# Attention and two expert layers on one core: the first layer's first expert chosen after four tiles, and zeros stored later

## The chip, the core and the metric

The kernel runs on one NeuronCore of a Trainium2 chip. Its engines are TensorE (PE, with its weight loads shown as PEld), VectorE (DVE), ScalarE (ACT), GpSimd (POOL) and SyncE (SP); each works off its own queue in program order, and they wait for each other by semaphores. Sixteen transfer (DMA) engines move data between HBM and the on-chip memory. The metric is the device time of one launch in microseconds.

## What is computed

A linear attention with decay over two sequences of 768 tokens and 8 heads, and two mixture-of-experts layers over the 1536 rows that it gives, with 8 experts of 512 x 1024 x 512 and one expert per row.

```python
state = gamma[None, :, None, None] * state + np.einsum('bhd,bhe->bhde', k[:, :, t], v[:, :, t])
y[:, :, t] = scale * np.einsum('bhd,bhde->bhe', q[:, :, t], state)
...
logits = x @ w_gate
expert_idx = np.argmax(logits, axis=1)
...
h = np.maximum(xe @ w1[e], 0.0)
ye = h @ w2[e]
out[mask] = gate_w[mask, None] * ye
```

The second layer does the same with weights of its own, and keeps at most `capacity` = 384 rows per expert.

## The kernel before

**Attention** goes over twelve tiles of 128 tokens (`n` from 0 to 11, alternating between the two sequences): scores, the state's update, the output `xt` from past and present, and `combine`, which transposes a tile's output back to rows and makes the gate's logits. ScalarE's queue stores each tile's rows and logits into the HBM tensor `x1d` (`a_store`).

**Routing** finds for every row its expert and its rank among that expert's rows. The first eight tiles do this in batches (`BATCHES`: five tiles and three), whose steps `pick`, `count`, `rank`, `slots` and `place` are set by hand between the tiles' steps; the last four tiles go one by one (`route_tile`). `run` keeps running counts. After eight tiles `early` gathers the first 128 rows of one expert, the "first" one, so that products with it can start before attention has ended. Before, layer 1's first expert is expert 0 by decree; layer 2's is the one with most rows by then (`choose`, which leaves a mask `one`, a bonus `first` and a floor `floor`, and the number in `chosen`; `of_first` picks that expert's column with the mask).

**An expert layer** is eight slots, each an expert with a fixed number of columns (`CAPS`), wide slots first: `finish_route` sorts the experts by their counts, with the first expert pinned to slot 0 by its bonus. If an expert has more rows than its slot, a conditional block at the end of the program does the rest. Slot 0 makes its hidden products with undivided weights (`whole`, line L429), 128 columns ahead of the others: the first batch from the rows of `early`, the second (`second`, from line L370's transposes on) when the remaining rows have been gathered with the index list `ig`. All else uses weights split in a high part `whi` (ScalarE, L163) and a rest `wlo` (VectorE or GpSimd, L174): 32 pairs of products per slot for the hidden side (L788 and L789) and 32 for the output side (L814 and L815).

**Weights** are loaded on SP's queue in pieces of 512 KB (`refill` into four buffers `st`, `load_whole`); a piece can be loaded when its buffer's last piece has been split. `know` gives the list of pieces an expert's number, fixed or read into a register of SP. The loads of slot 1 wait until the second gather of slot 0 has landed (`held`).

**`x2d`**, the rows of layer 2, has to be zero where layer 1 gives nothing. SP stores twelve tiles of zeros into it behind the last weight load of attention, and layer 1's scatters wait for them. `between(j, i)` is what stands beside part `i` (0 to 7) of slot `j`.

## Time and profile before

| | |
|---|---|
| median of 3 runs | 442.85 us (441.76 to 446.3) |
| profiled execution | 443.88 us; span 442.1 us, 1.8 us around it |
| PE | 411.3 us busy, 93% of the span |
| VectorE, ScalarE, GpSimd | 74%, 54%, 29% of the span |
| transfers | 100.50 MB, 227 GB/s in the mean |
| attention, with first products | to 71.7 us |
| slot 0 of layer 1 | from 77.5 to 98.9 us |
| layer 2 | from some 265 us on |

All times are from the start of the span. A row of the timeline gives start, length, engine, line, operation, output from inputs, and in brackets how long the engine stood idle before and what it waited for. The granted clock is the share of TensorE's full clock, 2.4 GHz, that was passed in a stretch; 0.50 is 1.2 GHz.

### The profile page before, as it was taken

The page shows a single profiled execution, that of the slowest core. Times are in us where ns is not written, and L with a number is a line of the kernel's source. Part 1 is how long each engine was busy: PE and PEld are TensorE (multiplying, and loading weights), DVE is VectorE, ACT ScalarE, POOL GpSimd, SP SyncE. Part 2 cuts the span into 40 slices and gives each one's busy share as a digit, 9 for nine tenths or more (in the row PEclk, how much of TensorE's full clock was granted, in tenths as well). Part 3 has the DMA queues.
Part 4 walks back from the last instruction along what each step waited for, and adds up shares of the span by engine and source line. Part 5 has one row for each costly group of instructions (what it writes and reads, how often), then busy time and mean ns, then how long its engine had stood idle before and what let it go on. Part 6 is the DMA issues. An engine that isn't in the chain of part 4 may idle for free.

```text
span 442.1 us, 9412 instructions
## 1 busy us (share of the span) xinstructions
PE 411.3 (93%) x3373; PEld 384.4 (87%) x3373; DVE 325.3 (74%) x858; ACT 239.2 (54%) x493; POOL 127.0 (29%) x102
## 2 busy tenths in 40 slices
PE   8999884998999999999999999998999999999980
PEld 7887674998899999999989898997888999999970
DVE  3658896177989898989899877187586877887830
ACT  2111240266757666667666651366676777878730
POOL 2443113033353535344442204003202303201020
PEclk9999999799999999999999999999999999999996
DMA  8998994628575766666665733559758677777510
GB/s 317 391 310 300 380 387 148 215 97 264 189 257 169 240 212 241 215 234 220 231 218 191 266 128 89 231 191 313 271 184 269 221 261 249 256 245 247 188 43 14
DMA packets 32854, 100.50 MB, mean 227 GB/s; under 512 B 5008, under 2 KB 5520, under 8 KB 32800
## 3 DMA queue, kind: packets, MB, share of 16 engines
q1 hardware_dynamic: 25488, 82.75, 54.1%
q0 software_dynamic: 5008, 13.06, 8.8%
q10 hardware_dynamic: 2304, 4.02, 2.4%
q8 instruction: 28, 0.46, 0.4%
q14 instruction: 26, 0.21, 0.2%
HBM read 87.08 MB, written 13.05 MB: 226 GB/s over the span
## 4 chain that ended last, share of the span: by engine, by line
PE 59%; DVE 16%; DMA 10%; issue 9%; ACT 2%; POOL 1%; POOLq 0%; SPq 0%; ACTq 0%; DVEq 0%
PE y L814 14%; PE h L788 13%; PE y L815 6%; PE h L789 6%; DVE wlo L174 5%; PE h L429 4%; PE cb L1277 4%; DMA vk<-vkr 2%; DMA whole<-w 2%; DVE hs L774 2%; PE tp L359 2%; DVE h L800 2%; DMA rows<-x1d,eig 2%; DVE rkey L209 2%; PE o L829 1%
## 5 line engine op out<-in xcount | busy, mean ns | idle before, releaser
L174 DVE TENSOR_TENSOR wlo<-st,whi 128x1024 fp32r<-128x1024 f32 x107 | 141.2, 1328 | 0.9 <-ACT whi L163 0.9
L163 ACT CAST whi<-st 128x1024 fp32r<-128x1024 f32 x120 | 124.8, 1045 | 25.4 <-DMA st<-w 24.5
L788 PE MATMUL h<-x,whi 128*128 128x416 f32 (+10 forms) x416 | 123.5, 364 | 0.0
L814 PE MATMUL y<-h,whi 128*128 128x416 f32 (+8 forms) x384 | 117.6, 370 | 0.0
L789 PE MATMUL h<-x,wlo 128*128 128x208 f32 (+10 forms) x416 | 104.5, 251 | 0.0
L815 PE MATMUL y<-h,wlo 128*128 128x208 f32 (+8 forms) x384 | 97.3, 253 | 0.0
L788 PEld LDWEIGHTS h<-x,whi 128*128 128x128 f32 x416 | 78.1, 188 | 2.5 <-issue 0.4
L789 PEld LDWEIGHTS h<-x,wlo 128*128 128x128 f32 x416 | 79.5, 191 | 0.1
L814 PEld LDWEIGHTS y<-h,whi 128*128 128x128 f32 x384 | 72.1, 188 | 2.4 <-issue 0.2
L815 PEld LDWEIGHTS y<-h,wlo 128*128 128x128 f32 x384 | 73.4, 191 | 0.0
L174 POOL TENSOR_TENSOR wlo<-st,whi 128x1024 fp32r<-128x1024 f32 x13 | 34.9, 2684 | 57.7 <-ACT whi L163 51.3
L318 POOL DMA_INDIRECT out<-ob,is x14 | 13.9, 995 | 114.8 <-ACT ob L835 111.1
L800 DVE SCALAR_TENSOR_TENSOR h<-hs,h 128x416 fp32r<-128x416 f32 (+10 forms) x52 | 29.0, 558 | 20.7 <-ACT h L799 17.9
L799 ACT ACTIVATE h<-hs 128x416 fp32r<-128x416 f32 (+10 forms) x52 | 27.1, 521 | 31.1 <-DVE hs L774 30.5
L774 DVE TENSOR_TENSOR hs<-h,hb 128x208 f32<-128x208 f32 (+10 forms) x104 | 32.0, 347 | 6.5 <-ACT hb L773 4.8
L429 PE MATMUL h<-x,whole 128*128 128x128 f32 (+1 forms) x256 | 32.4, 288 | 0.0
L318 POOL DMA_INDIRECT x2d<-row,is x16 | 16.5, 1031 | 55.3 <-ACT row L1290 27.6
L429 PEld LDWEIGHTS h<-x,whole 128*128 128x128 f32 x256 | 31.3, 202 | 0.4 <-issue 0.2
L773 ACT COPY hb<-h 128x208 f32<-128x208 f32 (+10 forms) x104 | 28.8, 316 | 4.0 <-PE h L789 2.2
L1288 ACT COPY row<-cb 128x512 f32<-128x512 f32 x11 | 6.4, 585 | 38.9 <-DVE lgb L1283 29.2
L774 DVE TENSOR_TENSOR yt<-y,yb 128x220 f32<-128x220 f32 (+8 forms) x48 | 15.1, 355 | 14.7 <-ACT yb L773 14.7
L829 PE MATMUL o<-whi,h 128*128 128x512 f32 (+1 forms) x64 | 24.3, 380 | 0.0
(185 smaller groups left out, 604.8 us busy)
## 6 DMA issues: line engine op xcount, KB each, us to landing
st<-w SPq DMA_DIRECT2D x120, 512.0 KB, 4.2
vk<-vkr SPq DMA_DIRECT2D x11, 512.0 KB
whole<-w SPq DMA_DIRECT2D x8, 512.0 KB, 8.4
x2d<-zero SPq DMA_DIRECT2D x12, 260.0 KB, 5.8
qb<-qT SPq DMA_DIRECT2D x12, 256.0 KB, 6.8
x1d<-row ACTq DMA_DIRECT2D x11, 260.0 KB, 4.5
kt<-kT SPq DMA_DIRECT2D x11, 256.0 KB, 5.3
vk<-vkr ACTq DMA_DIRECT2D x1, 512.0 KB
```

What stands on the lines that cost most here:

```text
L163: A.copy(hi, st)
L174: (eng or V).tensor_sub(lo, st, hi)
L318: ins = nc.gpsimd.indirect_dma_start(dst.rearrange("n (i d) -> (n i) d", i=parts) if parts > 1 else dst[:, :], bass.IndirectOffsetOnAxis(a ...
L429: T.matmul(ps[:, j], w[:, k, j % 2 * P:(j % 2 + 1) * P], x[:, k], start=k == 0, stop=k == KD - 1, skip_group_check=True)
L773: A.copy(b, ps[:, 1, :])
L774: V.tensor_add(out, ps[:, 0, :], b)
L788: T.matmul(ps, hi[:, k, fs], x[:, k, :, :cap], start=k == 0, stop=False, skip_group_check=True)
L789: T.matmul(ps[:, 0, :], lo[:, k, fs], x[:, k, 0, :cap], start=False, stop=k == KD - 1, skip_group_check=True)
L800: V.scalar_tensor_tensor(h[:, sl, 1, :cap], s, 0.0, h[:, sl, 0, :cap], ALU.max, ALU.subtract)
L814: T.matmul(ps[i], hi[:, ds], h[:, f, :, :cap], start=f == 0, stop=False, skip_group_check=True)
L815: T.matmul(ps[i][:, 0, :], lo[:, ds], h[:, f, 0, :cap], start=False, stop=f == KF - 1, skip_group_check=True)
L829: T.matmul(p, h[:, f, 0, ts_], hi, start=f == 0, stop=False)
```

## The change

Layer 1's first expert becomes the one that leads after four tiles: `choose` runs in the eighth tile (`n` = 7) on the running count, and SP reads its number ahead of the first weight loads (`know_first`). The first batch of routing has four tiles, the second four; the first batch's steps come one tile earlier, and its count and rank fall into one tile. Slot 0 gets 240 columns in place of 220, slots 1 to 5 get 220, 208, 200, 192 and 188 in place of 236, 220, 208, 200 and 192. The zeros of `x2d` are stored beside slot 0 of layer 1. Ahead of the transposes of slot 0's second batch stand 24 products of ones whose result is overwritten.

```diff
-CAPS = ((220, 236, 220, 208, 200, 192, 184, 176), (256, 256, 232, 208, 184, 168, 160, 128))
+CAPS = ((240, 220, 208, 200, 192, 188, 184, 176), (256, 256, 232, 208, 184, 168, 160, 128))
...
-BATCHES = ((0, 5), (5, 8))
+BATCHES = ((0, 4), (4, 8))
...
-    know(0, 0)
-
     at_ = {"load": 0, "hi": 0, "lo": 0}
...
-        V.tensor_add(key, nt, rt.get("first", con("first")))
+        V.tensor_add(key, nt, rt["first"])
...
-    def first_x(rows):
+    def first_x(rows, warm=0):
+
...
         for ks in range(0, 2), range(2, 4):
-            tp = mmtile("tp").rearrange("p (k c) -> p k c", k=KD)[:, 0:2, :cnt]
+            tp = mmtile("tp")
+            for _ in range(0 if ks[0] else warm):
+                T.matmul(tp[:, 0:P], ones16, ones16, start=True, stop=True)
+            tp = tp.rearrange("p (k c) -> p k c", k=KD)[:, 0:2, :cnt]
...
-    def choose(rin, li):
+    def choose(rin, li, S):
...
-        T.matmul(nt, ones16, rin["S"], start=True, stop=True)
+        T.matmul(nt, ones16, S, start=True, stop=True)
...
     def of_first(rin, a, dt, name):
...
-        if "one" not in rin:
-            return a[:, 0:1]
         junk = rp.tile([P, E], F32, tag="of", name="oj")
...
-        V.tensor_tensor(most, nt, rin.get("floor", con("floor")), ALU.max)
+        V.tensor_tensor(most, nt, rin["floor"], ALU.max)
...
         for n in range(NT):
+            if n == first + 1:
+                many[0][1]()
             a_scores(n)
...
             if n:
                 a_past(n - 1)
+            if n == first + 1:
+                many[0][2]()
             if n == first + 2:
-                many[0][2]()
+                know_first = choose(rt1, 0, run[:, BATCHES[0][1], :])
             if n == second + 1:
                 many[1][2]()
-                many[1][3](3)
+                many[1][3](4)
             a_state(n)
             if n == first:
                 many[0][0]()
-            if n == first + 1:
-                many[0][1]()
-            if n == first + 2:
+            if first < n < first + 3:
                 many[0][3](2)
-            if n == first + 3:
-                many[0][3](3)
...
             if n == NT - 4:
+                know_first()
                 refill(2)
...
-        for t in range(NT):
-            nc.sync.dma_start(x2d[t * P:(t + 1) * P, :], zero)
...
-            x[0] = first_x(rows[0][1])
+            x[0] = first_x(rows[0][1], 24)
             go(1)
...
-                    chosen.append(choose(rt[1], 1))
+                    chosen.append(choose(rt[1], 1, rt[1]["S"]))
...
             refill()
+            if li == 0 and j == 0:
+                for t in range(NT * i // 8, NT * (i + 1) // 8):
+                    nc.sync.dma_start(x2d[t * P:(t + 1) * P, :], zero)
```

How the instructions stand on two engines follows. On SP, at the end of attention, before (`st` and `whole` are weight pieces, `zero` is a tile of zeros, TENSOR_LOAD and ISA read a register):

```order
L485 DMA vk<-vkr 128x1024
L142 DMA st<-w 128x1024 x2
L154 DMA whole<-w 128x1024 x4
L142 DMA st<-w 128x1024 x2
L700 DMA x2d<-zero 128x520 x12
L283 TENSOR_LOAD order_1179
```

And the changed kernel's SP, at slot 0 of layer 1, where the zeros now stand (with buffer numbers; `w11` and `w12` are the two weight matrices):

```order
L138 DMA st_1310<-w11 128x1024
L138 ISA
L138 DMA st_1312<-w11 128x1024
L908 DMA x2d_72<-zero_166 128x520
L138 ISA
L138 DMA st_1324<-w11 128x1024
L138 ISA
L138 DMA st_1326<-w11 128x1024
L908 DMA x2d_72<-zero_166 128x520 x5
L138 ISA
L138 DMA st_1390<-w12 128x1024
L908 DMA x2d_72<-zero_166 128x520
```

The twelve stores have left the place between the first expert's weights and the sorted list's numbers, and stand behind and between the loads of slot 1.

On VectorE, in the tenth tile (`n` = 9), before (`bR` are the masks of `slots`, `bm` to `boh` the steps of `pick`, `run` those of `count`):

```order
L523 TENSOR_TENSOR wn_788<-du,wm_628 128x256
L611 TENSOR_SCALAR bR<-iota_79,r_123 128x256 x3
L584 TENSOR_REDUCE bm<-lgb 128x3
L585 TENSOR_TENSOR bk<-lgb,bm 128x24
L586 TENSOR_TENSOR bk<-bk,cs 128x24
L587 TENSOR_REDUCE bmk<-bk 128x3
L588 TENSOR_TENSOR boh<-bk,bmk 128x24
L593 TENSOR_TENSOR run<-run,boh 128x8 x3
L553 TENSOR_TENSOR xt<-ot,cs 128x256 x2
```

The changed kernel's VectorE in the same tile:

```order
L521 TENSOR_TENSOR wn_827<-du,wm_660 128x256
L582 TENSOR_REDUCE bm<-lgb 128x4
L583 TENSOR_TENSOR bk<-lgb,bm 128x32
L584 TENSOR_TENSOR bk<-bk,cs 128x32
L585 TENSOR_REDUCE bmk<-bk 128x4
L586 TENSOR_TENSOR boh<-bk,bmk 128x32
L591 TENSOR_TENSOR run<-run,boh 128x8 x4
L551 TENSOR_TENSOR xt<-ot,cs 128x256 x2
```

The three masks ahead of `pick` are gone, and one count more is there. In the eighth tile (`n` = 7) the changed kernel has `choose`, `ck` to `floor`:

```order
L1283 TENSOR_REDUCE lgb<-cb 128x8
L380 TENSOR_TENSOR ck<-ch,cs 128x8
L382 TENSOR_REDUCE cm<-ck 128x1
L384 TENSOR_SCALAR one_638<-ck,cm 128x8
L387 SCALAR_TENSOR_TENSOR cj,ce<-one_638,cs 128x8
L389 CAST chosen_643<-ce 128x1
L391 SCALAR_TENSOR_TENSOR first_645<-one_638,cs 128x8
L393 TENSOR_SCALAR floor_647<-one_638 128x8
L521 TENSOR_TENSOR wn_658<-du,wm_489 128x256
L609 TENSOR_SCALAR bR<-iota_79,r_123 128x256 x2
L551 TENSOR_TENSOR xt<-ot,cs 128x256 x2
```

Before, that tile had `wn`, five counts `run`, and `xt` there; now seven operations and two masks stand ahead of `xt`.

## Rows read from the trace of the kernel before

**Rows 1.** The page, part 1: busy time, share and instructions of each engine.

```profile
PE 411.3 (93%) x3373; PEld 384.4 (87%) x3373; DVE 325.3 (74%) x858; ACT 239.2 (54%) x493; POOL 127.0 (29%) x102
```

**Rows 2.** Chain of waits, 44 to 78 us: start, length, what.

```profile
45.93 9.22 DMA whole<-w
...
72.13 5.20 DMA rows<-x1d,ig
```

**Rows 3.** Timeline of PE: start, us, engine, line, operation; idle before it.

```profile
62.59 0.63 PE L370 MATMUL tp<-cs,rows 128*128 128x128 f32 x4 [0.96 <-DMA rows<-x1d,eig]
...
77.47 0.84 PE L370 MATMUL tp<-cs,rows 92*128 92x92 f32 x4 [5.79 <-DMA rows<-x1d,ig]
```

**Rows 4.** Stretches of 1 us: PE busy, granted clock, transfer share, GB/s.

```profile
66.00:67.00 1.00, 1.00 (x13) 1.00 1.05 377
...
75.00:76.00 1.00, 0.00 (x0) 0.64 0.24 83
...
81.00:82.00 1.00, 1.00 (x7) 0.50 1.04 254
...
90.00:91.00 1.00, 1.00 (x11) 1.00 0.00 0
```

**Rows 5.** Line L429, first products: 67 to 71.7, 78 to 82, 82 to 88.5 us.

```profile
L429 PE MATMUL h<-x,whole x41: 275/275/356, 66.8 to 71.4; 128*128 128x128 f32 x41
...
L429 PE MATMUL h<-x,whole x19: 361/421/481, 78.1 to 81.9; 128*128 128x92 f32 x11, 128*128 128x128 f32 x8
...
L429 PE MATMUL h<-x,whole x55: 274/275/421, 81.7 to 87.9; 128*128 128x92 f32 x55
```

**Rows 6.** Last store of x1d, index list, gather (timeline); landing of the thirteen stores (L560).

```profile
66.09 0.33 ACTq L560 DMA_DIRECT2D x1d<-row  x1
...
67.12 0.17 DVE L242 TENSOR_TENSOR ig<-tbp,tb 128x16 int32<-128x16 f32 x1 [0.53 <-PE cnt L245]
...
72.13 1.25 POOL L344 DMA_INDIRECT rows<-x1d,ig  x1 [15.64 <-DVE z L303]
...
DMA to landing us min/median/max: 3.6/4.8/5.9
```

**Rows 7.** Line L459, the forty products at the program's start.

```profile
L459 PE MATMUL warm<-ones x40: 289/314/314, 1.1 to 5.2; 128*128 128x128 f16 x40
```

**Rows 8.** Timeline of PE: first product of slots 1 to 5, and idle in slot 1.

```profile
98.93 0.38 PE L788 MATMUL h<-x,whi 128*128 128x472 f32 x1
...
106.58 0.35 PE L1277 MATMUL cb<-iw,yt 128*92 128x136 f32 x1 [1.13 <-ACT row L1290]
...
116.79 0.20 PE L222 MATMUL rk<-S,ones 128*92 128x8 f16 x1 [0.64 <-DVE S L226]
...
125.36 0.36 PE L788 MATMUL h<-x,whi 128*128 128x440 f32 x1
...
148.49 0.36 PE L788 MATMUL h<-x,whi 128*128 128x416 f32 x1
...
171.03 0.36 PE L788 MATMUL h<-x,whi 128*128 128x400 f32 x1
...
193.62 0.36 PE L788 MATMUL h<-x,whi 128*128 128x384 f32 x1
```

**Rows 9.** Timeline, VectorE and PE: attention's tiles eight and ten, and choose in layer 2.

```profile
36.81 0.42 DVE L523 TENSOR_TENSOR wn<-du,wm 128x256 f32<-128x256 f32 x1 [1.02 <-PE du L520]
...
46.31 1.05 DVE L611 TENSOR_SCALAR bR<-iota,r 128x256 f16<-128x256 f16 x3
...
50.19 1.05 PE L1277 MATMUL cb<-iw,xt 128*128 128x136 f32 x7 [1.47 <-DVE xt L553]
...
221.46 0.16 DVE L380 TENSOR_TENSOR ck<-ch,cs 128x8 f32<-128x8 f32 x1
...
222.47 0.17 DVE L393 TENSOR_SCALAR floor<-one 128x8 f32<-128x8 f32 x1
```

**Rows 10.** Timeline of ScalarE: a cast that waits for its weight load.

```profile
96.95 1.06 ACT L163 CAST whi<-st 128x1024 fp32r<-128x1024 f32 x1 [1.37 <-DMA st<-w]
```

More of the change, by code (lines that the diff above doesn't have):

```diff
@@ L67, in _consts @@
     put("tok", P * np.arange(NT)[None, :] + s[:, None])
-    put("first", np.broadcast_to(np.array([1e6] + [(E - e) / 16 for e in range(1, E)]), (P, E)))
     put("tie", np.broadcast_to((E - np.arange(E)) / 16, (P, E)))
@@ L73, in _consts @@
     put("held", np.broadcast_to(np.array(CAPS[1]), (P, E)))
-    put("floor", np.broadcast_to(np.array([P] + [0] * (E - 1)), (P, E)))
     cand = np.arange(P) // NM
```

## Prediction

> **What bounds the kernel now.** The page comes first: TensorE (PE) is busy for 93% of the span [rows 1], so two things can move the time: fewer or shorter products, and the few places where PE stands still. The chain of waits names the largest of those: a transfer of `rows` from `x1d`, 5.20 us long, that begins at 72.13 [rows 2]. It is the second row gather of layer 1's first expert; PE's timeline shows PE idle for 5.79 us until it lands, and idle for 0.96 us for the first gather at 62.59 [rows 3]. The stretches of one microsecond show the second half of that price: the granted clock goes from full (2.4 GHz) to 0.64 between 75 and 76, some 4 us after the last product, is still 0.50 (1.2 GHz) at 81 to 82 [rows 4]. The line of the first products shows what that does: at the low level 19 records start from 78.1 to 81.9 (0.207 us each), at the high one 55 from 81.7 to 87.9 (0.115 each) [rows 5].
>
> Why is that gather so late? Its index list was written at 67.29, but GpSimd starts it at 72.13. It reads `x1d`, whose last piece ScalarE's queue stores at 66.09, and such stores took 3.6 to 5.9 us to land [rows 6]. One of 5.6 us, within that range, ends at 71.7, 0.4 us before the gather. The transfer engines are full then (share 1.05, 377 GB/s at 66 to 67 [rows 4]), and what fills them are the twelve zero stores. So I read: zeros hold the row store, it holds the gather, that holds PE, and the pause costs the clock. In the slots behind, PE has almost no gap: the starts of the slots, 22 to 26 us apart, with the idle rows of slot 1 [rows 8], say that a slot's length goes with its width.
>
> **Zeros moved.** 12 x 128 x 520 x 4 B = 3.2 MB leave the end of attention, 8.5 us of transfer time at 377 GB/s. The stores of `x1d` then meet idle engines. I price the last store at the shortest of the 13 stores, 3.6 us, which was itself taken with engines busy; the bound above is the 5.6 us read off now. The Trainium skill (DMA: Bandwidth & Descriptors, Latency and other measured facts) puts the fixed cost of a transfer at about 2 us; by that estimate the store lands 1.6 us sooner still and the sum would end up to 1.2 us lower, because the thrown-away products (below) then hold PE. No row here shows a store on idle engines. The list needs a multiply with its accumulator read and a cast more (`of_first`), some 0.4 us by the pace of the eight like them in layer 2 (1.2 us [rows 9]), and is ready at 67.7, so the store still ends last. Gather start: 66.09 - 0.3 (attention, below) + 3.6 + 0.4 = 69.8; it lands 5.2 us later [rows 2], 0.1 more for 112 rows in place of 92: 75.1. PE goes on at **75.1 instead of 77.47: -2.4 us** (between -0.3 with no earlier store and -3.6 where the products bind).
>
> The zeros are now among the weight loads that SP issues beside slot 0: one after the second load, five after the fourth, the last six in pieces between the next six loads. The first six fall in a stretch where nothing moves (share 0.00 at 90 to 91 [rows 4]); they cost nothing. The other six are 1.6 MB, 4.2 us at 377 GB/s, between loads that ScalarE's cast does wait for (1.37 us at 96.95 [rows 10]). Each load passes at most two zeros, 1.4 us; later casts of the same slot come after their load by several microseconds. The first scatter into `x2d`, in GpSimd's queue, has to wait for all twelve; behind it stand a scatter and one split. I take **+0.4 us**, from 0 to 4.2.
>
> **Thrown-away products.** 24 of the 40 warm-up products' kind, which start every 0.105 us (40 from 1.1 to 5.2 [rows 7]): 2.5 us, from the end of the first batch at 71.7 - 0.3 = 71.4 to 73.9. The transposes behind them are ready at 75.1, so they cost nothing; if the gather landed at once they would cost 2.5. PE's pause shrinks from 5.8 to 1.2 us, far from the 4 us after which the clock fell. With full clock, the 72 records behind the gather take 72 x 0.115 = 8.3 in place of the 9.9 us from 78.1 to 87.9 and the last, and four transposes 0.63 in place of 0.84 [rows 3]: **-1.8 us**.
>
> **Slots by place.** Slot 0's second half is 112 wide, not 92. Its first products start every 0.115 us at 92 columns and at 128 alike (41 from 66.8 to 71.4 [rows 5]), so 20 columns more are free. The isolated spacing in the Trainium skill (TensorE: Matmul & The Clock Gate, Back-to-back issue gap: columns over 2.4 GHz) would charge 64 x 20 / 2.4 GHz = 0.5 us for them and the sum would be that much higher; this row says otherwise, and I follow the row. Its second matrix is 240 wide, not 220: 32 pairs; a slot's width costs 0.05 us per column for 64 pairs (slots 2 and 3: 23.13 and 22.54 us for 220 and 208 columns [rows 8]), so half of that x 20: **+0.5 us**. The other seven slots go from 236, 220, 208, 200, 192, 184, 176 to 220, 208, 200, 192, 188, 184, 176. Slot 1, now 26.43 us with 1.13 + 0.64 idle, becomes what slot 2 is, 23.13 plus the same 1.77 idle: -1.5. Slot 2 takes slot 3's 22.54: -0.6; slot 3: -0.3; slots 4 and 5: 12 columns x 0.05 = -0.6. **-3.0 us**. VectorE splits eight weight pieces per slot whatever its width; if that pace already rules, half of it is lost, hence -1.5 to -3.0.
>
> **The choice and the batches of four.** `choose` is new in attention's eighth tile: one small product, and seven VectorE operations that took 1.2 us in layer 2 (221.46 to 222.47 + 0.17 [rows 9]), ahead of `wn` and `xt`, for which PE waits. VectorE waits 1.02 us for PE in such a tile (36.81 [rows 9]), of which the two masks moved here take a part; I leave 0.7 as cover, so +0.5. All of it, 1.2, is the bound. Counting and ranking of the first batch now fall into one tile: +0.4. `early` has two multiplies more: +0.4; four masks for three in tile ten: +0.2. Against it, the tenth tile loses the three masks at 46.31 (1.05 us) that stood ahead of `xt`, where PE idled 1.47 us [rows 9], and gains one count: -0.9. The first gather's 0.96 us of idle ends with the full engines: -0.9. Sum **-0.3** (used above), bounds -1.9 and +1.6. SP loads the chosen number before the eight weight loads of the first expert, behind the last attention load. By my estimate from these tiles the number is there before SP is; the last whole piece lands at 55.2 [rows 2] and is used behind the transposes of 62.59 [rows 3], so a load later by a microsecond is hidden.
>
> **Sum.** -2.4 - 1.8 + 0.4 + 0.5 - 3.0 = -6.3. The profiled execution took 443.88 us: 437.6. It stood 1.03 above the median of 442.85, so against the median: **436.5**.
>
> **Rivals.** (a) *The gather doesn't come earlier.* The profile names VectorE's `z` as its releaser [rows 6], so `z` would end just ahead of it; if that is real, the gather stays at 72 and PE at 77.2. The products still bridge: idle 3.3 us, so the clock may hold. -0.3 - 1.8 + 0.4 + 0.5 - 3.0 = -4.2: 438.6; without the clock 440.4. Against it: the list was there at 67.3 and nothing in the code joins it to `z`. 0.15.
> (b) *The choice lengthens attention* by its whole 1.6 in place of -0.3: all behind it comes 1.9 later, 438.4. For it speaks that VectorE paces tile ten; against it, the slack in the tiles before. 0.12.
> (c) *The zeros slow the weights.* Place: SP's queue in slots 0 and 1. If each of the twelve delays a load that a cast waits for, 12 x 0.27 MB at 377 GB/s = 8.5 us go into slot 1's products: -6.7 + 8.5 = +1.8, **444.7, slower than before**. It decides once the loads' lead over their casts is used up; half of it gives 440.4. Against it: six zeros fall into an empty stretch. 0.10.
> (d) *The pauses and slot gains come in full*: store at 2 us, attention at -1.9: 433.7. 0.08.
> The forecast (435 to 438.5) has 0.55.
>
> **How the numbers follow.** A kernel like this can be told from no change at about 1%, 4.4 us: faster means below 438.4. The forecast lies below that but for 0.03 of it, (d) does, (a) and (b) half. 0.52 + 0.08 + 0.07 + 0.06 = 0.73. Slower by over 1% takes (c) in full with (b): 0.05. Same: 0.22. The range that holds 8 in 10 leaves out (d)'s lower end and the upper part of (c): 433 to 441.
>
> **What would show it.** In the changed profile: the gather of `ig` starting near 70 with the transfer share low at 63 to 70; 24 products in the pause and a clock of 1.00 from 70 to 90; first products at 0.115 us throughout; slot 1 near 25 us; zeros at 85 to 94 with casts no later relative to PE. Slot 1 longer than 25 us would speak for (c), cb rows of the attention tiles further apart than 4.3 to 5.2 for (b), and a gather still at 72 for (a). I'd be wrong altogether if a slot overflowed, since the conditional block would run: the reference's inputs give 213 rows to the expert that leads after four tiles (73 of 512) and 206, 203, 196, 188, 183, 180, 167 to the others, all within the new widths.

## The result and the profile after

The changed kernel took 440.38 us (median of 16 runs, 436.78 to 442.39), the kernel before 444.72 beside it (16 runs, 441.76 to 452.22). The ratio is 0.9918, 95% interval 0.9893 to 0.9943: 0.8% faster, some 3.6 us, where the forecast was 1.4%. The ratio is taken over fast runs and leaves out three slow ones of the kernel before (450.90 to 452.22 us), so it isn't the quotient of the two medians. The profiled execution took 437.99 us, span 436.2. That is 5.9 less than the profiled execution before and looks like the forecast of 6.3, but it is one of the shorter ones, and its sum is made of other terms than mine.

The front comes first. On PE's timeline the 24 products now stand in the pause, no row of the transposes behind them shows idle time (5.79 us in [rows 3]), and slot 0's second matrix starts at 83.47. The last line is its first product before, at 88.01:

```profile
50.59 1.62 PE L1277 MATMUL cb<-iw,xt 128*128 128x136 f32 x7 [1.78 <-DVE xt L551]
...
73.77 1.50 PE L367 MATMUL tp<-ones 128*128 128x128 f16 x24
75.11 0.56 PE L370 MATMUL tp<-cs,rows 112*128 112x112 f32 x4
...
83.47 0.46 PE L811 MATMUL y<-h,whi 128*128 128x480 f32 x1
...
88.01 0.45 PE L814 MATMUL y<-h,whi 128*128 128x440 f32 x1
```

The list, the gather and the last store of `x1d` answer to [rows 6]; they are from the timelines of VectorE and GpSimd and from the store's and the gather's own lines. A landing row is minimum, median and maximum; the first is the gather's, the second the last store's:

```profile
69.84 0.15 DVE L404 CAST ig<-of 128x1 int32<-128x1 f32 x1
70.80 1.00 POOL L340 DMA_INDIRECT rows<-x1d,ig  x1 [12.31 <-DVE at L268]
...
DMA to landing us min/median/max: 3.3/3.3/3.3
...
L558 ACTq DMA_DIRECT2D x1d<-row x1: 331/331/331, 67.5 to 67.5; - x1
...
DMA to landing us min/median/max: 2.1/2.1/2.1
```

The last store is issued at 67.45 and lands in 2.1 us, at 69.5 (the one before it took 1.8). The list, written at 70.0, is now what the gather waits for, and the gather takes 3.3 us instead of 5.2. The stretches of one microsecond (PE busy, granted clock, transfer share, GB/s; as [rows 4]) show idle transfer engines at 70 to 71 and full clock at 76 to 81, but a fall of the clock where before had none, in attention's tile ten behind the idle 1.78 us of the first row above. The last line is before, during its own gather: the engines were idle there too, so the shorter gather isn't explained by idle engines (more under before_zeros_early).

```profile
50.00:51.00 1.00, 0.41 (x3) 0.96 0.92 330
51.00:52.00 1.00, 1.00 (x6) 0.50 1.04 413
...
70.00:71.00 1.00, 1.00 (x12) 1.00 0.00 0
76.00:77.00 1.00, 1.00 (x12) 1.00 1.10 336
80.00:81.00 1.00, 1.00 (x12) 1.00 1.05 420
...
72.00:73.00 1.00, 0.00 (x0) 1.00 0.00 0
```

Then the slots, as [rows 8]: first products of slots 1, 2, 3, 4 and 7, and the idle rows of slot 1. The last line is slot 7's first product before.

```profile
94.88 0.36 PE L785 MATMUL h<-x,whi 128*128 128x440 f32 x1
102.53 0.72 PE L1277 MATMUL cb<-iw,yt 128*112 128x136 f32 x4 [1.17 <-ACT row L1290]
113.98 0.21 PE L218 MATMUL rk<-S,ones 128*112 128x8 f16 x1 [2.18 <-DVE S L222]
122.20 0.36 PE L785 MATMUL h<-x,whi 128*128 128x416 f32 x1
144.76 0.36 PE L785 MATMUL h<-x,whi 128*128 128x400 f32 x1
167.34 0.36 PE L785 MATMUL h<-x,whi 128*128 128x384 f32 x1
235.22 0.41 PE L785 MATMUL h<-x,whi 128*128 128x352 f32 x1
...
239.21 0.41 PE L788 MATMUL h<-x,whi 128*128 128x352 f32 x1
```

Slot 1 is 27.32 us long (94.88 to 122.20), though 16 columns narrower than the 26.43 before. From slot 1's start to slot 7's start it is 140.34 us; before it was 140.28 (98.93 to 239.21). The whole gain of the slots is missing. The idle 2.18 us in slot 1 has a chain that GpSimd's rows, VectorE's and those of the last zero store give; the last line is the first scatter before:

```profile
109.13 1.04 POOL L314 DMA_INDIRECT x2d<-row,is  x1 [11.70 <-DVE rm L203]
110.47 0.98 POOL L314 DMA_INDIRECT x2d<-row,is  x1 [0.30 <-issue]
111.45 2.38 POOL L170 TENSOR_TENSOR wlo<-st,whi 128x1024 fp32r<-128x1024 f32 x1
...
111.38 2.48 DVE L221 TENSOR_SCALAR E<-roh,tk 128x8 f16<-128x8 f16 x1
113.78 0.15 DVE L222 TENSOR_TENSOR S<-S,roh 128x8 f16<-128x8 f16 x1
...
L908 SPq DMA_DIRECT2D x2d<-zero x1: 423/423/423, 101.6 to 101.6; - x1
...
DMA to landing us min/median/max: 6.1/6.1/6.1
...
106.88 1.04 POOL L318 DMA_INDIRECT x2d<-row,is  x1 [4.68 <-ACT row L1290]
```

The last zero store is issued at 101.58 and lands 6.1 us later, at 107.70. The first scatter into `x2d`, whose row is there at 102.5, waits until 109.13, 1.43 us behind that landing; in widths_before and products_none below it starts 1.43 us behind the last landing too. Behind the scatters in GpSimd's queue stands a weight split. It starts at 111.45 and runs until 113.83, and VectorE's operation on eight columns (`E`) that began at 111.38 ends with it, after 2.48 us. PE's rank product waits for what VectorE does next.

### The profile page after: what moved, and what is told of

Same layout as the page of the kernel before. It is cut to its first block, busy times and chain, and to the rows that moved or that the text cites. A ratio compares the mean times of both kernels' runs of the same rounds, so it can differ in the third digit from the quotient of the medians.

```text
span 436.2 us, 9492 instructions
## 1 busy us (share of the span) xinstructions
PE 410.6 (94%) x3398; PEld 383.4 (88%) x3398; DVE 327.4 (75%) x873; ACT 238.3 (55%) x493; POOL 126.1 (29%) x102
## 4 chain that ended last, share of the span: by engine, by line
PE 47%; DVE 28%; issue 10%; ACT 5%; DMA 5%; POOL 1%; SPq 0%; POOLq 0%; ACTq 0%; DVEq 0%
PE y L811 10%; DVE wlo L170 10%; PE h L785 9%; PE y L812 4%; PE h L427 4%; PE cb L1277 4%; PE h L786 4%; DVE hs L771 3%; DVE h L797 3%; ACT h L796 2%; DMA st<-w 2%; DVE rkey L205 2%; DMA rows<-x2d,igs 2%; DMA vk<-vkr 1%; PE o L826 1%
## 5 line engine op out<-in xcount | busy, mean ns | idle before, releaser
L811 PE MATMUL y<-h,whi 128*128 128x416 f32 (+9 forms) x384 | 116.7, 369 | 0.2 <-DVE h L797 0.2
L812 PE MATMUL y<-h,wlo 128*128 128x208 f32 (+9 forms) x384 | 96.8, 252 | 0.0
L427 PE MATMUL h<-x,whole 128*128 128x128 f32 (+1 forms) x256 | 30.5, 277 | 0.0
L427 PEld LDWEIGHTS h<-x,whole 128*128 128x128 f32 x256 | 29.3, 192 | 0.6 <-issue 0.5
L771 DVE TENSOR_TENSOR yt<-y,yb 128x208 f32<-128x208 f32 (+9 forms) x48 | 15.0, 353 | 14.1 <-ACT yb L770 14.1
```

The costliest lines, as they stand in the source:

```text
L427: T.matmul(ps[:, j], w[:, k, j % 2 * P:(j % 2 + 1) * P], x[:, k], start=k == 0, stop=k == KD - 1, skip_group_check=True)
L771: V.tensor_add(out, ps[:, 0, :], b)
L811: T.matmul(ps[i], hi[:, ds], h[:, f, :, :cap], start=f == 0, stop=False, skip_group_check=True)
L812: T.matmul(ps[i][:, 0, :], lo[:, ds], h[:, f, 0, :cap], start=False, stop=f == KF - 1, skip_group_check=True)
```

## Experiments

All are timed in five rounds beside the kernel before (ratios are against it); the medians of before in the five groups were 444.72, 444.29, 444.05, 444.56 and 446.01. "Slot 1" is from its first product to slot 2's, in the profiled execution, and "idle" the one ahead of the rank product of its second half (in widths_before ahead of a `y` product right behind).

| version | median us | ratio, interval | slot 1 us | idle, us |
|---|---|---|---|---|
| the change | 440.38 | 0.9918 (0.9893 to 0.9943) | 27.32 | 2.18 |
| the change, again | 440.99 | 0.9906 (0.9869 to 0.9943) | 30.41 | 2.48 |
| zeros_back | 438.59 | 0.9879 (0.9826 to 0.9933) | 25.90 | 0.75 |
| zeros_early | 436.53 | 0.9834 (0.9790 to 0.9878) | 26.50 | 0.76 |
| widths_before | 440.96 | 0.9923 (0.9894 to 0.9952) | 30.78 | 2.19 |
| products_none | 438.34 | 0.9887 (0.9837 to 0.9938) | 29.71 | 2.09 |
| early_no_products | 437.43 | 0.9855 (0.9816 to 0.9894) | 26.84 | 0.75 |
| early_widths_before | 437.75 | 0.9877 (0.9834 to 0.9919) | 26.46 | 0.70 |
| split_vector | 438.21 | 0.9881 (0.9841 to 0.9921) | 26.67 | 0.65 |
| before_zeros_early | 439.08 | 0.9897 (0.9862 to 0.9932) | 27.30 | 0.70 |
| early_counts_later | 436.98 | 0.9852 (0.9814 to 0.9891) | 26.02 | 0.75 |
| early_counts_split | 436.36 | 0.9821 (0.9785 to 0.9858) | 25.90 | 0.52 |
| early_number | 435.81 | 0.9770 (0.9725 to 0.9815) | 26.24 | 0.75 |
| early_number_counts | 436.35 | 0.9781 (0.9735 to 0.9828) | 26.41 | 0.76 |
| early_pieces_counts | 436.64 | 0.9772 (0.9721 to 0.9823) | 26.45 | 0.76 |

### Where the zeros stand

**zeros_back**: the change with the zeros back at the end of attention.

```diff
+        for t in range(NT):
+            nc.sync.dma_start(x2d[t * P:(t + 1) * P, :], zero)
...
-            if li == 0 and j == 0:
-                for t in range(NT * i // 8, NT * (i + 1) // 8):
-                    nc.sync.dma_start(x2d[t * P:(t + 1) * P, :], zero)
```

> The changed kernel with the twelve zero stores back at the end of attention. Theory A (the zeros beside slot 0 hold the first scatter into x2d, it holds the split behind it on GpSimd, and slot 1 pays): the first scatter starts within 1 us of its row, slot 1 takes near 25 us in place of 27.3, but the gather of ig waits again for the last row store, PE goes on 2 to 4 us after its products; the two nearly cancel, ratio to the kernel before 0.99 to 1.00. Theory B (slot 1 is paced by VectorE's eight splits whatever the zeros do): slot 1 stays near 27 us, and the late gather comes on top: 1.00.

**zeros_early**: the zeros beside slot 0, but all in its parts 1 to 3, four in each.

```diff
-            if li == 0 and j == 0:
-                for t in range(NT * i // 8, NT * (i + 1) // 8):
+            if li == 0 and j == 0 and 0 < i < 4:
+                for t in range(4 * i - 4, 4 * i):
```

> The changed kernel with all twelve zero stores beside parts 1 to 3 of slot 0, four each, ahead of the fifth weight load of slot 1. Theory A: all zeros have landed by about 92, the first scatter starts with its row near 103, GpSimd's split comes near 106 and VectorE's small operations are not held in front of the rank; slot 1 near 25 us, total 2 us below the changed kernel, ratio 0.987. Theory B: slot 1 stays at 27 us, ratio 0.992.

With the zeros back, PE waits 2.44 us for the gather's rows and the clock is at half from 77 to 81; that is what is left of the pause in which before lost its time, and moving the zeros away takes it out. But slot 1 is then 25.90, and the version is no slower than the change: what the move gains in front it gives back in slot 1. With early zeros both are had, and the version came out better than expected (3.9 us under the change by the medians, 2 expected). GpSimd's rows of zeros_early, and PE's:

```profile
102.92 1.03 POOL L314 DMA_INDIRECT x2d<-row,is  x1 [5.95 <-ACT row L1290]
106.57 0.98 POOL L314 DMA_INDIRECT x2d<-row,is  x1 [2.62 <-PE h L786]
107.71 3.02 POOL L170 TENSOR_TENSOR wlo<-st,whi 128x1024 fp32r<-128x1024 f32 x1 [0.16 <-ACT whi L159]
...
112.65 0.21 PE L218 MATMUL rk<-S,ones 128*112 128x8 f16 x1 [0.76 <-DVE S L222]
```

The scatter starts when its row is there, 6.2 us sooner, and the split ends before VectorE comes to `E`.

### The stall itself

**split_vector**: the change, zeros late, with slot 1's first split on VectorE.

```diff
-POOL = (((1, 5),) * (E - 1) + ((),), ((),) * E)
+POOL = (((1, 5), (5,)) + ((1, 5),) * (E - 3) + ((),), ((),) * E)
```

> The changed kernel with its late zeros, and the first weight split of slot 1 on VectorE in place of GpSimd, whose queue the zeros hold there. Theory: the stall of 2.2 us in slot 1 comes from GpSimd's late split running beside VectorE's small operation ahead of the rank product; without that split the idle row before the rank product shrinks to below 0.8 and slot 1 is 1.4 us shorter: 438.9 against 440.38, ratio 0.988. Rival (the rank product is late because the row's transfer or the scatter is late, whichever engine splits): the idle of 2.2 us stays, 440.4 or, with one split more on VectorE (1.1 us), 441.5, ratio 0.992 to 0.995.

**after_again**: the changed kernel itself.

> The changed kernel once more, unaltered, for another profiled execution of it. Theory: the stall of 2.2 us ahead of the rank product of slot 1 is there in every execution, since it comes of the order of GpSimd's queue, and so slot 1 is again longer than 27 us; stretches of half clock behind a pause come and go between executions. 439 to 441, ratio 0.992. Rival (the stall was an accident of the one execution): slot 1 near 25.5 us with an idle row of 0.6 to 0.8.

In split_vector the zeros are as late as in the change and the scatters too (111.31, 114.04). Only the split is gone from GpSimd's queue, and with it the stall:

```profile
113.33 0.39 DVE L221 TENSOR_SCALAR E<-roh,tk 128x8 f16<-128x8 f16 x1
...
113.80 0.21 PE L218 MATMUL rk<-S,ones 128*112 128x8 f16 x1 [0.65 <-DVE rro L225]
```

So the late scatter does hardly any harm by itself (`E` took 0.39 us in place of 0.22); the split behind it does. 438.21 lies 0.7 us from the theory's number; of the 1.4 us expected in slot 1 only 0.65 came, since PE waits 0.91 us for `yt` early in this slot, a wait that the execution shown first doesn't have. Run again, the change has the stall again, and this time TensorE's granted clock falls behind it as well. VectorE, PE, and the one-microsecond stretches of after_again:

```profile
113.85 2.78 DVE L221 TENSOR_SCALAR E<-roh,tk 128x8 f16<-128x8 f16 x1
...
116.75 0.26 PE L218 MATMUL rk<-S,ones 128*112 128x8 f16 x1 [2.48 <-DVE S L222]
...
116.00:117.00 1.00, 0.25 (x3) 0.79 0.00 0
117.00:118.00 1.00, 1.00 (x5) 0.50 0.30 66
120.00:121.00 1.00, 1.00 (x8) 1.00 0.88 238
```

Slot 1 took 30.41 us here. In three of the four profiled executions with late zeros and the split on GpSimd (this one at 116.6 to 120.0, widths_before at 115.9 to 119.3, products_none at 112.4 to 115.8) the clock fell in slot 1; in none of the twelve without the stall did it. The execution shown first was the one of the four in which it did not, and its 437.99 lies below the median; this one, 442.00 us, lies above, but the clock fell in its attention too.

### Widths

**widths_before**: the change with the widths of before in slots 1 to 7. **early_widths_before**: the same on zeros_early.

```diff
-CAPS = ((240, 220, 208, 200, 192, 188, 184, 176), ...
+CAPS = ((240, 236, 220, 208, 200, 192, 184, 176), ...
```

> The changed kernel with slots 1 to 5 of layer 1 as wide as before (236, 220, 208, 200, 192; slot 0 keeps 240). Theory A (slot length goes with width at 0.05 us per column, and the gain was only hidden by the stall in slot 1): slots 1 to 5 together 2.4 to 3 us longer, ratio 0.998. Theory B (VectorE's pace sets the slots, the width nothing): within 0.5 us of the changed kernel, ratio 0.992.

> Zeros in parts 1 to 3 of slot 0, and the other seven slots as wide as before (236, 220, 208, 200, 192, 184, 176). Theory: widths count where nothing stalls: 0.05 us per column and slot gave a forecast of 3.0 us for them; the stall in slot 1 swallowed it. Expected: 2.4 to 3 us above the version with early zeros (436.53), 439.2, ratio 0.990. Rival (VectorE's splits or the weights pace slots 1 to 3, so the width counts for nothing): 436.5, ratio 0.983.

On the change the widths made no difference (440.96 against 440.38). The stall is there with another victim: the split (112.82, 2.41 us) meets the making of `rR`, which takes 3.17 us, and PE waits 2.19 us for `h` behind it:

```profile
112.15 3.17 DVE L227 TENSOR_SCALAR rR<-iota,r 128x256 f16<-128x256 f16 x1
```

Without the stall the medians are 1.2 us apart (437.75 against 436.53), between theory and rival, though the two intervals overlap. In the two profiled executions slots 1 to 6 took 140.26 us with the old widths and 139.51 with the new, 0.75 less. Slot 1: 26.46 and 26.50. Slot 2: 23.13 and 22.55. Slot 3: 22.56 and 22.59. Slot 4: 22.58 and 22.20. Slot 5: 22.17 and 22.41. Slot 6: 23.36 and 23.26. What becomes of saved columns shows in slot 3's row of rank products, in zeros_early and then in early_widths_before:

```profile
158.06 0.20 PE L218 MATMUL rk<-S,ones 128*80 128x8 f16 x1 [0.35 <-DVE S L222]
```

```profile
158.52 0.20 PE L218 MATMUL rk<-S,ones 128*92 128x8 f16 x1
```

With 200 columns PE waits 0.35 us for VectorE's `S`, with 208 it does not. In slots 2 and 4 the column price of 0.05 us came out (0.58 and 0.38 us less, 0.6 and 0.4 forecast). In slot 1 the narrower version waits 0.63 us for `yt`, which the wider one doesn't; why slot 5 is 0.24 us longer stays open.

### Products

**products_none**: the change without the 24 products. **early_no_products**: zeros_early without them. They enter no output.

```diff
-            x[0] = first_x(rows[0][1], 24)
+            x[0] = first_x(rows[0][1])
```

> The changed kernel without the 24 thrown-away products. Theory A (with the zeros gone from there the gather has landed within 1.3 us of PE's last product, so there is no pause left to bridge): same time, granted clock full from 75 on, ratio 0.992. Theory C (the products are what keeps the clock): PE idles over 3 us, first products start every 0.2 us for some microseconds, 2 us more, ratio 0.996.

> Zeros in parts 1 to 3 of slot 0, and the 24 thrown-away products left out (they enter no output). Theory: with the row store landing in 1.8 us and the list ready at 70.8, the gather lands as the products end, so they bridge nothing and cost up to 24 x 0.056 = 1.3 us. Expected against the version with early zeros (436.53): 1.0 us less, 435.5, ratio 0.981 +- 0.004. Rival (the products keep TensorE's granted clock up in the pause): without them a stretch of half clock behind the pause, as in the kernel before at 75 to 82.5, and 2 us more: 438.5, ratio 0.988.

Without them PE waits 0.28 us (products_none) and 0.35 us (early_no_products) for the gather, and the clock holds behind it in both. The products took 1.34 us (0.056 each, against 0.105 in [rows 7]) and bridge a pause that is no longer there. Their price doesn't show in the times: one median is 2 us lower without them, the other 0.9 higher.

### The choice and the rest

**before_zeros_early**: the kernel before, with the zeros as in zeros_early and nothing else changed.

> The kernel before with one thing changed: the twelve zero stores go into parts 1 to 3 of slot 0; no choice, batches of five and three, slot widths as before, no products added. Theory: the zeros' place is nearly the whole gain (gather earlier by 1.5 us or more, no stretch of half clock behind it, no stall in slot 1), and choice, batches and widths together are worth about 1 us: 437.5, ratio 0.985. Rival (the choice and its narrower slots carry 3 us, as forecast): 439.5, ratio 0.990 or above. Against both: if the gather's pause without products costs the clock again, 441, ratio 0.993, with a granted clock of 0.50 behind 75.

439.08: the move of the zeros alone is worth 1.0%, and what the version with early zeros has beyond it (choice, batches, widths, products) some 2.5 us by the medians, though the two intervals overlap a little. That is nearer to the rival (439.5) than to the theory (437.5). Three rows matter. Without the choice PE still waits 2.66 us for the gather, but the clock holds. The gather itself takes 5.25 us (chain of waits, first row). And in tile ten the clock is at half here too, with no choice and batches of five and three:

```profile
70.04 5.25 DMA rows<-x1d,ig
...
75.43 0.51 PE L373 MATMUL tp<-cs,rows 92*128 92x92 f32 x4 [2.66 <-DMA rows<-x1d,ig]
...
51.00:52.00 1.00, 1.00 (x8) 0.50 1.04 419
76.00:77.00 1.00, 1.00 (x11) 1.00 0.62 112
```

So the half-clock stretch in attention needs neither the choice nor the batches of four. The gather says what the move of the zeros doesn't do: it is as long here as before, where the engines were idle too, and 3.3 to 3.5 us in every version with the choice, zeros_back among them. So its 1.9 us come with the choice (and the batches of four, which every version has that has the choice). Two things change there: the list stands in a tile of its own (`ig<-of`, 128x1, where before it is a column of `ig`, 128x16 in [rows 6]), and it names the rows of another expert. No run tells the two apart. From the first batch's end to slot 0's second matrix it is 16.3 us before, 11.0 here, 9.5 in zeros_early: the zeros' place is worth some 5.3 us of that front, the choice some 1.5, both without what attention itself took.

**early_counts_later**: zeros_early, with the second batch's counts behind the ninth tile's output products, to shorten the 1.78 us of idle time there. **early_counts_split**: this and split_vector in one.

```diff
             if n == second:
                 many[1][0]()
-                many[1][1]()
             if n:
                 a_out(n - 1)
+            if n == second:
+                many[1][1]()
```

> Zeros in parts 1 to 3 of slot 0, and in attention's ninth tile the second batch's four counts (0.75 us on VectorE) issued behind that tile's output products instead of ahead of them. Theory: PE waits there 1.8 to 2.1 us for xt, which VectorE makes behind the batch's choice and counts; in three of five executions with the change the granted clock fell to half right behind that wait. With the counts moved the wait is 1.0 to 1.3 us and the clock holds: against the version with early zeros (436.53) 0.5 us less for the wait and 0.7 for a fall of the clock in half the executions, 435.3, ratio 0.981. Rival (VectorE paces these tiles, so the 0.75 us comes back ahead of the next tile's product): 436.5, ratio 0.983, with PE waiting longer at the next cb or rk row.

> All three mends in one: zeros in parts 1 to 3 of slot 0, the second batch's counts behind the ninth tile's output products, slot 1's first weight split on VectorE. Theory: with the zeros early GpSimd's queue is free, so the split's engine no longer matters, and only the counts are left to gain: as the version with early zeros and late counts (436.98), 436.5 to 437, ratio 0.984; the split on VectorE may cost up to 1 us in slot 1. Rival (GpSimd's split still disturbs VectorE's small operations with early zeros): slot 1 below 26.0 us and 435.5, ratio 0.981.

The wait fell from 1.95 us in zeros_early to 0.47, but the counts account for only half of that, 0.75 us. Another 0.70 is `boh`, the step ahead of them: in zeros_early it stands beside GpSimd's `vp` (47.44 to 48.48) and ends with it after 0.89 us, here `vp` waits 1.92 us for its load and `boh` takes 0.19. The medians didn't fall (436.98 and 436.36 against 436.53). One thing that attention then meets shows in after_again: ScalarE's cast (first row) and PE:

```profile
61.32 1.05 ACT L159 CAST whi<-st 128x1024 fp32r<-128x1024 f32 x1 [2.01 <-DMA st<-w]
...
65.10 1.03 PE L1308 MATMUL cb<-iw,xt 128*128 128x136 f32 x4 [1.98 <-ACT x L371]
...
66.00:67.00 1.00, 1.00 (x7) 0.50 0.38 131
...
45.11 0.89 SPq L138 DMA_DIRECT2D st<-w  x2
```

SP issues the weight loads at 45.1, behind its load of the chosen number; before, it issued them at 43.20. In this execution ScalarE comes to the casts before the weights, and PE waits 2 us for ScalarE. early_counts_later has a cast that waits too (1.87 us at 59.77), but that execution, 434.42 us, is the fastest of its six: that this wait is why the medians stood still isn't shown. With the split on VectorE as well (early_counts_split) slot 1 is 25.90, as its rival said, and the time 436.36, as its theory said.

**early_number**: zeros_early with that load one tile earlier, ahead of the last attention loads. **early_number_counts**: with the later counts too. **early_pieces_counts**: and with the four pieces that ScalarE casts loaded ahead of the whole ones.

```diff
+            if n == NT - 5:
+                know_first()
             step(n - 2, 0)
             if n == NT - 4:
-                know_first()
                 refill(2)
```

> Zeros in parts 1 to 3 of slot 0, and SP's load of the chosen expert's number one tile earlier, ahead of the last attention tile's loads instead of behind them. Theory: the number is there at 38.1, SP reads it only at 44 and thereby issues the eight weight loads 1.9 us later than before; ScalarE's casts at 61 to 63 wait for them in some executions, and PE behind ScalarE. Expected: first weight load at 43.2 to 44 instead of 45.1, no cast between 58 and 64 that waits for st, and up to 1 us less in the median, 435.5 to 436.5, ratio 0.981. Rival (the loads' start doesn't matter, the casts wait because attention's own loads fill the engines): casts as late as before, 436.5 or more, ratio 0.983.

> The same with the second batch's counts behind the ninth tile's output products too. Theory: the counts' version had its tile-nine wait down from 1.9 to 0.47 us but then met the late weights (casts waiting 1.87 us); with both mended attention ends 1 to 2 us earlier: 435.0, ratio 0.980. Rival (the weights' landing takes 8 us from 44 whatever is done, so attention's end is set by transfers): 436.5 to 437, ratio 0.983, with a cast still waiting over 1 us.

> The same again, with the four pieces that ScalarE casts loaded ahead of the four whole pieces in place of around them. Theory: the third and fourth piece, issued at 51.2 to 52.2 behind the whole ones, are what the casts at 59 to 63 wait for; loaded first they are there by 54, no cast waits behind 55, and PE's wait for ScalarE's x at 65 is gone: 434.5 to 435.5, ratio 0.979. Rival (the whole pieces then come late for the first products, behind 66): PE waits for a whole piece after 66 and the time is 437 or more.

In early_number the first weight load is issued at 42.97 and no cast waits for `st` in that stretch:

```profile
42.97 0.89 SPq L138 DMA_DIRECT2D st<-w  x2
...
60.61 1.99 ACT L159 CAST whi<-st 128x1024 fp32r<-128x1024 f32 x2 [0.40 <-ACT row L1289]
```

435.81 us, ratio 0.977: the fastest of all, though it, zeros_early and the two behind it (436.35, 436.64) can't be told apart by these intervals. The two behind it missed their theories (435.0, and 434.5 to 435.5); in early_number_counts casts still wait, 0.44 and 0.85 us. Against the kernel before it is 2.3% less, against the changed kernel 1.0% by the medians and 1.5% by the ratios. In early_pieces_counts no cast waits either, and yet the clock was at half from 53.9 to 60.7, with no wait of PE over 0.8 us ahead of it in that tile or the one before. What makes the clock fall in attention stays open.

## Why the prediction was right and wrong

**The gather and the clock behind it: right, by another sum.** Forecast 2.4 + 1.8 = 4.2 us; slot 0's second matrix starts 4.54 earlier. The parts differ. The store landed in 2.1 us, not 3.6: that no row of before showed, and the Trainium skill (DMA: Bandwidth & Descriptors, Latency and other measured facts) had it with its 2 us. The gather took 3.3 us, not 5.2; this came with the choice and not with the zeros, and the forecast had no such term. Both gains were more than I counted, and attention, 2.2 us later, took most of the surplus. That PE went on at 75.11, the forecast's 75.1, is luck: the added products held it by then, and the gather had landed at 74.1. The step to the clock rested on a pause of 1.2 us as safe. PE had no pause here, so this run doesn't test it; elsewhere the clock fell behind waits of 1.78 us (tile ten) and 2.44 us (zeros_back), and not behind 2.66 us (before_zeros_early).

**Attention: the -0.3 failed.** The last tile's work came 2.2 us later (the first batch ends at 73.9 instead of 71.7). About half of that, 1.2 us, is the half clock of tile ten, 3.4 us at 0.50, and not the choice's: from this tile's first row of `cb` to the next tile's it is 6.99 us, and 5.82 or 5.83 in zeros_back, products_none and after_again, whose clock holds there; before it is 5.19, in before_zeros_early with half clock 6.39. Choice and batches leave 1.0. In the five executions without such a stretch, of versions whose attention is the changed kernel's, the last tile's first `cb` product stands at 63.6 to 65.5, before at 63.8: they cost from -0.2 to 1.7 us there. Of the sum's terms, choice and counting came out (PE reaches tile ten's `du` 1.0 us later, 0.9 forecast), and so did most of the 0.9 for the masks gone from tile ten (from `du` to `cb` 4.44 us in place of 5.02); the stretch behind it, 0.6 longer, is what the masks and `early` were put at together. What failed is the first gather's -0.9: its 0.96 us of idle went, but PE waits 1.04 us for VectorE's `lg` in its place, and from `cb` to `cb` around it the time is 3.94 us, before 3.93. And "a load later by a microsecond is hidden" was wrong: the loads came 1.9 us later, and after_again paid 2 us of wait and half clock at 65 to 69 for it.

**Slots by place: the -3.0 failed, and most of the difference between forecast and result is here.** Two things took it: the stall below, which the change itself has, and a mis-sized term, which shows where there is no stall. The term is a column's price of 0.05 us, taken from slots 2 and 3 and applied to slots 2 to 5, and for slot 1 the whole difference to slot 2, which is 0.1 us per column. The price holds where PE is last (slot 2: -0.58, forecast -0.6; slot 4: -0.38, forecast -0.4). In slot 3 VectorE's `S` is late next, and PE waits instead of multiplying; slot 1 without its waits went from 24.66 (before) to 23.94 (zeros_early), 0.7 and not 1.5. In all the widths gave 0.75 us in one pair of executions. I had named that case (VectorE's pace) and let it take half; there it took three quarters.

**Zeros: the step that failed is the one on GpSimd's queue.** I wrote that the first scatter waits for all twelve zeros and that a scatter and one split stand behind it, and then priced only the weight loads, +0.4. The zeros did hold the scatter, by 6 us; the split slid with it to where VectorE makes the rank's operand; 2.2 us of idle PE came of it and, in three of four executions, 3.4 us at half clock, some 1.5 us more by my estimate (slot 1 of products_none and after_again, 29.71 and 30.41 against 27.32, less another wait of 0.95 and 1.33). Slot 1 is over the 25 us that I named as the sign for rival (c), but (c)'s mechanism, casts behind late loads, isn't the stall: split_vector leaves zeros and loads as they are and the stall goes. Something like (c) may have a smaller part: in four of the five executions with late zeros PE waits 0.9 to 1.3 us for `yt` early in slot 1, in after_again behind a cast that stood 3.84 us for its load. Early zeros show such waits too (0.3 to 1.0 in seven of nine), so what they owe to the zeros is not shown. The placement costs about 4 us in the medians (440.4 to 441.0 against 436.5 with early zeros), 3.2 to 3.7 by the ratios; split_vector gets back some 2.2 to 2.8 of them by the medians and 1.1 to 1.6 by the ratios, where its interval overlaps the change's. The rest I can't place.

**Slot 0 and products.** The second half's 20 columns were free as read off [rows 5]: 64 records of 112 columns start every 0.11 us. Slot 0's second matrix took 11.41 us for 10.92: +0.49, the forecast +0.5. The products had nothing to bridge: the rows were there at 70.80 + 3.3 = 74.1, the transposes began at 75.1, so they held PE 1.0 us in that execution; the medians don't show it. They had been priced at 0.105 us each and took 0.056.

The sum by the profiled executions: front -4.5, slot 0 +0.5, slots 1 to 6 +0.1, behind them -0.2, and 1.7 us in the program's last microseconds, where nothing was changed. That stretch is 11.1 to 11.6 us in thirteen of the sixteen profiled executions, this one among them, and 12.8 to 13.1 in three, the kernel before among them: chance, as far as is known. Without it the 5.9 is 4.1. A fall of the clock in slot 1, which this execution was spared, takes more where it comes; how often it comes in the runs without a profile is not on record, so how the 3.6 us of the medians is made up isn't shown to the last term.

## What to carry to other kernels

Moving a transfer off one wait puts it ahead of another: follow every queue that waits for it, and ask of each instruction behind that wait what it will run beside when it comes late. A price per column, read from stages where one engine is last, holds only until the next engine is last; read the idle rows of each stage before multiplying. A load whose address is computed on the chip comes later than the one it replaces, here by 1.9 us.

## What the runs showed of the hardware

An operation of VectorE on eight elements per partition took 2.48 us instead of 0.22 because a split ran on GpSimd: each ended when the split did (111.45 + 2.38 = 113.83; 111.38 + 2.48 = 113.86). In slots 2 to 6 of this execution the operation beside a split is the one that makes `rkey`, 1.62 to 1.66 us for 0.23, and it ends with the split to 0.02 us. In zeros_early it is so in slot 1 (1.60 us; the split ends at 107.71 + 3.02), while `hs`, which reads one operand from PSUM (0.67 us for two), and the reduction `rm` (0.15) beside the same split took no longer than elsewhere:

```profile
108.39 0.67 DVE L771 TENSOR_TENSOR hs<-h,hb 128x220 f32<-128x220 f32 x2
108.98 0.15 DVE L203 TENSOR_REDUCE rm<-row 112x1 f32<-112x8 f32 x1
109.17 1.60 DVE L205 SCALAR_TENSOR_TENSOR rkey<-row,rm,cs 112x8 f32<-112x8 f32 x1
```

The Trainium skill (SBUF — State Buffer, SBUF: two separate sides) says that VectorE and GpSimd share a pair of ports as "an exclusive lock, not a bandwidth split", which an operation of VectorE needs in a two-port mode or with two SBUF inputs, and that the one that comes second is blocked for the other's whole instruction. The trace agrees that such operations end with the split, 2.48 and 1.60 us for what take 0.22 and 0.23 alone. Who comes second can't be read off the starts: the record of `E` begins 0.07 us ahead of the split's, in after_again 0.37 us. I hadn't weighed this rule; it would have spoken against this placement, once one sees that the split slides.

Two more such meetings show in these traces. In the changed kernel a split of VectorE that began at 142.13 beside one of GpSimd (141.37 to 143.76) took 2.72 us, where one at 140.06 took 1.22, and it ended 1.1 us behind the other: there the split on GpSimd saved VectorE little. And in attention's tile ten `boh` took 0.72 to 1.03 us beside GpSimd's `vp` in six executions, and 0.19 in after_again and early_counts_later, where the two do not meet.

The 24 products of 128 columns in f16 took 0.056 us each, where the same kind took 0.105 at the program's start, with a granted clock of 1.00 in both stretches. A store of 128 KB landed in 1.8 us with the transfer engines idle (share 0.00) and in 5.6 us with them full (share 1.05, kernel before).
